# Fillers set by TensorE's trailing load, table loads begun in pauses, rounding moved to VectorE, and a new order of a fused attention and feed-forward kernel

## The chip, the cores and the metric

One core of a Trainium2 chip. The metric is the device time of one execution in microseconds, as the median of several runs. TensorE (PE) multiplies matrices, VectorE (DVE) and ScalarE (ACT) work on tiles, GpSimd (POOL) does some additions, and SyncE (SP) issues the DMAs. L748 is line 748 of the kernel.

## The reference

Inputs are q, k, v of 4 batches, 8 heads, 576 positions, 64 per head, and two weights of 512 x 2048 and 2048 x 512, all float32.

```python
q_d, k_d, v_d = (a.reshape(B, H, Sd, 4, D).mean(axis=3) for a in (q, k, v))
out_up = np.repeat(sm_attn(q_d, k_d, v_d), 4, axis=2)
mask = np.abs(pos[:, None] - pos[None, :]) < 4
scores = np.where(mask, scale * np.matmul(q, k.transpose(0, 1, 3, 2)), -1e9)
out_local = np.matmul(softmax(scores), v)
x = (out_up + out_local).transpose(0, 2, 1, 3).reshape(B * S, H * D)
h = x @ w_in
g = h * np.tanh(softplus(h))
return g @ w_out
```

So there are two attentions, one over means of four positions and one over a band of seven neighbours; their sum goes through two dense layers with Mish between them. 2304 rows of 512 come out.

## The kernel before

Work comes in units of one batch and one pair of heads, 16 in all. A unit loads q and k (`qk`) and v (`vv`), sums groups of four (L391), computes coarse scores `sc` (L406) and band scores `sl` (L445, some with the mask added by a matmul, L440), takes both softmaxes, transposes the probabilities (`at` with the remainder `Ar` at L489 and L490, `pt` and `pve` at L517 and L523), evicts them on ScalarE (`AT` L493, `R` L496, `PT` L520 and L524), multiplies by the values (`pvo` L504 and L508, the band's products L532), adds both on VectorE (L545) and splits the result into a rounded word and its remainder (L563 on ScalarE, L565 on VectorE). The remainder block `R` is 96 x 2 x 144 with three blocks of 16 rows on its diagonal; three ScalarE copies write them, and the rest was set to zero once.

Each weight tensor of 128 x 512 arrives as 64-bit words; ScalarE and VectorE turn their halves into one float (L596, L598, L600), ScalarE rounds the float to a high word (L603), and VectorE subtracts for the low word (L604). A product of two such split numbers is three matmuls.

The dense layers go in columns of 384 rows (`c`) and blocks of 128 hidden features (`f`, 16 of them). For columns 0 and 1 a slot is one (c, f): twelve matmuls into a hidden bank `h` (L748), of which there are two; Mish on ScalarE (L772), the rounded word `g` (L774), the remainder on VectorE (L775), and nine matmuls into three output banks `acc` (L788). The later columns are done four at a time by a scheme with seven products instead of eight (L709, L716).

The four units of batch 0 are the prologue; they use their own tiles and banks. The dense layers' banks and the weights with f of 5 and more take memory that the prologue leaves. The other units are spread over the first 32 slots. Exp and Mish need different tables on ScalarE; a table load stands before the first instruction that needs another table.

No order is written by hand. `Plan.order` (L162) runs through all operations with assumed durations and emits, per engine, the ready operation of the lowest priority number; each engine then executes its queue in that order. Priorities come from constants at the top: `ATT` and `UNIT` for the units, `WPRI`, `WACT` and `WDMA` for weights, `LAG` for output groups behind their slot. Where TensorE has nothing ready, the planner may insert a filler, a matmul of 128 x 512 on the identity (L885) into a bank that is used for nothing. Whether it does so was decided by the columns multiplied so far in the running period of fixed length `TICK` of the planner's time:

```python
o, when = None, max(1700, min((k + 1) * TICK, k * TICK + hot.get(k, 0) * TICK / (PACE * BUSY) - 299))
if when <= t < 1e6:
    o, when = self.fill(t), t + 100
```

Of the kernel before, what the change touches and what calls it, by code (L numbers as in the profile page):

```python
# [19 lines left out]
P = 128  # L20
BIG = 1e30
CH = 384
LAG = (5.03, 6.42, 5.0)
FA = 5
SETS = 3
ATT = {0: (-811.4, 62.2), 1: (-43.2, 13.7), 2: (1.5, 0.3), 3: (9.2, 7.8)}
WPRI = (-7.19, 1.09, 7.26)
UNIT = {(0, 0): 6, (0, 2): -4, (1, 2): 3, (0, 3): 20, (1, 0): -3, (1, 3): -29, (1, 1): 10, (0, 1): -22, (3, 2): -4, (3, 3): -1, (2, 1): 2, (2, 0): -9, (2, 2): 3, (2, 3): 7, (3, 0): -1, (3, 1): 3}
WARM = True
NPRO = 4  # L30
WACT = 33
# [6 lines left out]
PMASK = (0,)  # L38
AMUL = ((1, 0), (1, 2), (1, 3))
AEXP = ((0, 2), (1, 0), (1, 3))  # L40
NMISH = (4,)
TAIL = 0
SPRE = 34
SPRE2 = 65
JPRE = 17
XDMA = 2
QPRE = 36
QPRE2 = 87
QSTEP = 0.6
QDMA = -37  # L50
SUMS = 2
TPRE = 49
UPRE = -7
KEEP = 50
LOAD = 1350
TICK, BUSY, PACE = 3413.3, 3060, 1.6
KW = 38
RATE, LAND = 415.0, 1100
PAGE, FIRST, FETCH = 256, 193, (3200, 6000)
# [34 lines left out]
class Plan:  # L94
# [59 lines left out]
    def heat(self, hot, t, dur, cols):  # L154

        k = int(t // TICK)
        while dur and k * TICK < t + dur:
            part = min(t + dur, (k + 1) * TICK) - max(t, k * TICK)
            hot[k] = hot.get(k, 0) + cols * part / dur
            k += 1  # L160

    def order(self):  # L162
        import heapq
        for o in self.ops:
# [7 lines left out]
        dma, hot, parked, gap = 0.0, {0: 1000}, {}, 0  # L172
# [5 lines left out]
        while events:  # L178
# [3 lines left out]
            for e in pending:  # L182
# [12 lines left out]
                while ready[e]:  # L195
# [34 lines left out]
                    if e == "pe":  # L230
                        k = int(t // TICK)
                        if hot.get(k - 1, 0) < BUSY:
                            dur = o.cold
# [8 lines left out]
                        self.heat(hot, t, dur, o.cols)  # L242
                        for b in o.bufs:
                            b.todo -= 1
                    elif e == "act" and o.tab and o.tab != tab:
                        dur, tab = dur + max(0, LOAD - (t - free[e])), o.tab
# [3 lines left out]
                    if e == "sp":  # L250
                        late = t > 1e5
                        dma = max(dma, t + LAND + 400 * late) + o.dur * (1 + 0.28 * late)
                        free[e], end = max(t + 420, dma - DQ), dma
# [25 lines left out]
                if e == "pe" and self.filler and free[e] <= t:  # L279
                    k = int(t // TICK)  # L280
                    o, when = None, max(1700, min((k + 1) * TICK, k * TICK + hot.get(k, 0) * TICK / (PACE * BUSY) - 299))
                    if when <= t < 1e6:
                        o, when = self.fill(t), t + 100
# [4 lines left out]
                    if o:  # L288
                        o.end = free[e] = t + (o.cold if hot.get(k - 1, 0) < BUSY else o.dur)
# [27 lines left out]
class Kernel:  # L317
# [10 lines left out]
    def consts(self, pool):  # L328
# [625 lines left out]
```

## Time and profile before

| | us |
|---|---|
| median of 3 runs | 511.86 (511.3 to 512.08) |
| the profiled execution | 512.84 |
| its span, first to last instruction | 511.1 |
| TensorE busy in it | 490.2 |
| VectorE busy | 357.9 |
| ScalarE busy | 293.3 |

The profile is of one execution. Times in it count from the first instruction, and the execution's own time is 1.7 us longer than the span. Busy time is the union of an engine's instructions; two neighbouring instructions overlap a little, so the mean of one is longer than its distance to the next. PEclk is the granted TensorE clock, 1.00 for 2.4 GHz and 0.50 for 1.2 GHz.

### The profile page before, as it was taken

Reading aid. Unit: us, or ns where it says so; the run is one execution under the profiler, and the core shown is the slowest. Engines: PE = TensorE matmul, PEld = TensorE weight load, DVE = VectorE, ACT = ScalarE, POOL = GpSimd, SP = SyncE. Lnnn points to the kernel's source line nnn. Section 1 sums busy time; section 2 is a strip of 40 time slices with the busy share of each in tenths; the row PEclk is TensorE's granted clock in tenths of the full one; section 3 lists DMA queues with packets and bytes.
Section 4 is the critical chain, followed back from the end, with each engine's and each line's share of the span. In section 5 each row is a group of like instructions: output and inputs, shape, how many; then the busy total and the mean of one; then the engine's idle time right before and its main releaser. Section 6 shows DMA issues by size and latency. Waiting matters only on the chain.

```text
span 511.1 us, 11643 instructions
## 1 busy us (share of the span) xinstructions
PE 490.2 (96%) x4743; PEld 416.4 (81%) x4743; DVE 357.9 (70%) x804; ACT 293.3 (57%) x708; POOL 40.5 (8%) x62
## 2 busy tenths in 40 slices
PE   8788899999999999999999999999999999999997
PEld 3555778787977888887788988899888998889885
DVE  5796599999646676657898885666948676566442
ACT  2597799979855665856574433344735444344422
POOL 6400120010101111101100000000000000000000
PEclk9995899999999999999999999999999999999999
DMA  8974999240543677744230320100512000000003
GB/s 347 415 283 145 381 379 380 79 172 1 172 131 85 230 245 261 240 156 167 75 107 17 104 84 17 31 1 15 140 39 101 0 1 0 2 0 1 0 1 123
DMA packets 23381, 65.60 MB, mean 128 GB/s; under 512 B 2592, under 2 KB 12832, under 8 KB 21280
## 3 DMA queue, kind: packets, MB, share of 16 engines
q1 hardware_dynamic: 23328, 64.86, 35.4%
q8 instruction: 37, 0.61, 0.5%
q14 instruction: 16, 0.13, 0.1%
HBM read 53.84 MB, written 11.01 MB: 127 GB/s over the span
## 4 chain that ended last, share of the span: by engine, by line
PE 71%; ACT 12%; DVE 7%; DMA 6%; issue 2%; SPq 1%; POOL 0%; ACTq 0%; POOLq 0%; DVEq 0%
PE acc L788 32%; PE h L709 22%; PE h L748 7%; DMA raw_wi<-in_w_in_dram 3%; PE pve L532 3%; ACT A L413 2%; DMA vv<-in_vv_dram 1%; ACT raw_wo L596 1%; ACT L413 1%; PE pt L517 1%; DMA qk<-in_qk_dram 1%; ACT L772 1%; PE warm L885 1%; PE sc L406 1%; ACT raw_wi L596 1%
## 5 line engine op out<-in xcount | busy, mean ns | idle before, releaser
L788 PE MATMUL acc<-wo,g 128*128 128x512 f32 x864 | 223.7, 395 | 0.0
L788 PEld LDWEIGHTS acc<-wo,g 128*128 128x128 f32 x864 | 159.0, 188 | 26.8 <-issue 0.6
L716 DVE TENSOR_TENSOR u<-h,u 128x384 f32<-128x384 f32 x112 | 61.7, 554 | 30.9 <-PE h L709 30.2
L748 PE MATMUL h<-x,wi 128*128 128x384 f32 x384 | 79.1, 348 | 2.8 <-ACT mA L772 2.3
L748 PEld LDWEIGHTS h<-x,wi 128*128 128x128 f32 x384 | 68.0, 192 | 8.4 <-ACT mA L772 4.4
L772 ACT ACTIVATE u<-u 128x384 f32<-128x384 f32 (+1 forms) x66 | 33.9, 515 | 52.9 <-DVE u L716 52.9
L775 DVE TENSOR_TENSOR g<-u,g 128x384 fp32r<-128x384 f32 (+1 forms) x66 | 35.8, 543 | 38.5 <-ACT g L774 38.4
L774 ACT ACTIVATE g<-u 128x384 fp32r<-128x384 f32 (+1 forms) x66 | 33.8, 514 | 37.2 <-PE acc L788 36.3
L681 ACT ACTIVATE t<-b 128x256 fp32r<-128x256 f32 x64 | 26.3, 416 | 43.9 <-PE h L709 40.5
L709 PE MATMUL h<-x,t 128*128 128x384 f32 x192 | 41.3, 339 | 1.0 <-DVE u L716 1.0
L709 PE MATMUL h<-x,wi 128*128 128x384 f32 x192 | 40.4, 338 | 0.0
L709 PEld LDWEIGHTS h<-x,t 128*128 128x128 f32 x192 | 34.5, 188 | 4.1 <-DVE u L716 1.7
L478 POOL TENSOR_TENSOR vv<-vv 128x512 f32<-128x512 f32 x16 | 21.2, 1322 | 201.9 <-DMA vv<-in_vv_dram 167.1
L709 PEld LDWEIGHTS h<-x,wi 128*128 128x128 f32 x192 | 34.5, 188 | 2.2 <-issue 0.2
L709 PE MATMUL h<-sfar,t 128*128 128x384 f32 x144 | 31.3, 336 | 0.0
L678 DVE TENSOR_TENSOR b<-b,b 128x256 f32<-128x256 f32 x64 | 27.0, 422 | 1.1
L709 PEld LDWEIGHTS h<-sfar,t 128*128 128x128 f32 x144 | 25.7, 188 | 2.1
L672 DVE TENSOR_TENSOR b<-wi 128x256 f32<-128x256 f32 x64 | 26.3, 421 | 1.0
L391 DVE TENSOR_REDUCE qkd<-qk 128x288 f32<-128x1152 f32 x16 | 21.4, 1339 | 7.9 <-DMA qk<-in_qk_dram 7.8
L682 DVE TENSOR_TENSOR t<-b,t 128x256 fp32r<-128x256 f32 x64 | 26.5, 416 | 0.0
L532 PEld LDWEIGHTS pve<-PT,vv 38*64 38x64 f32 x640 | 22.4, 145 | 4.5 <-issue 1.2
L775 DVE TENSOR_TENSOR g<-mA,g 128x384 fp32r<-128x384 f32 x32 | 18.7, 587 | 8.7 <-ACT g L774 8.6
(106 smaller groups left out, 699.1 us busy)
## 6 DMA issues: line engine op xcount, KB each, us to landing
vv<-in_vv_dram SPq DMA_DIRECT2D x16, 1152.0 KB, 5.8
qk<-in_qk_dram SPq DMA_DIRECT2D x16, 582.0 KB, 6.5
raw_wi<-in_w_in_dram SPq DMA_DIRECT2D x16, 512.0 KB, 10.8
raw_wo<-in_w_out_dram SPq DMA_DIRECT2D x16, 512.0 KB, 9.9
out_dram<-o SPq DMA_DIRECT2D x18, 256.0 KB, 2.2
sa<-far SPq DMA_DIRECT2D x16, 192.0 KB, 2.7
fars<-sa SPq DMA_DIRECT2D x16, 192.0 KB, 1.9
q<-fars SPq DMA_DIRECT2D x16, 192.0 KB, 2.8
```

Of the source, the lines that this page charges most:

```text
L532: nc.tensor.matmul(o_()[64 * h:64 * h + 64, c0:c0 + 32], vw()[64 * e:64 * e + KW, j, f, 64 * h:64 * h + 64], PT()[64 * e:64 * e + KW, j, 6 ...
L672: op("dve", dve(n), lambda k=k, w=w, c=c: nc.vector.tensor_tensor(out=t[k](), in0=w()[:, 0, c:c + n].bitcast(F32), in1=w()[:, 1, c:c + n]. ...
L678: op("dve", dve(n), lambda ko=ko, a=a, b_=b_: nc.vector.tensor_tensor(out=t[ko](), in0=t[a](), in1=t[b_](), op=ALU.subtract), r=[t[a], t[b ...
L681: op("act", act(n), lambda w=w, ko=ko: nc.scalar.activation(w()[:, 0], t[ko](), AF.Copy), r=[t[ko]], w=[(w, 0)])
L682: op("dve", dve(n), lambda w=w, ko=ko: nc.vector.tensor_tensor(out=w()[:, 1], in0=t[ko](), in1=w()[:, 0].bitcast(F32), op=ALU.subtract), r ...
L709: nc.tensor.matmul(bank()[:, :CH], wv(a, j), xv()[:, b_], start=j == 0 and m == 0, stop=j == 1 and m == 2)
L716: op("dve", dve(CH), lambda: nc.vector.tensor_tensor(out=at[to](), in0=bank()[:, :CH], in1=at[a](), op=ALU.add), r=[bank] + u[a] * (a != t ...
L748: nc.tensor.matmul(h()[:, :CH], w()[:, a, kt * P:(kt + 1) * P], x()[:, b_, :], start=kt == 0 and j == 0, stop=kt == 3 and j == 2)
L772: op("act", act(n, psum), lambda o_=o_: nc.scalar.activation(Gv()[:, o_], Hv()[:, o_], AF.Mish), r=h_, w=x_, tab="mish")
L774: op("act", act(n), lambda o_=o_: nc.scalar.activation(g()[:, 0, o_], Gv()[:, o_], AF.Copy), r=x_, w=[one])
L775: op("dve", dve(n), lambda o_=o_: nc.vector.tensor_tensor(out=g()[:, 1, o_], in0=Gv()[:, o_], in1=g()[:, 0, o_].bitcast(F32), op=ALU.subtr ...
L788: nc.tensor.matmul(a_(), g()[:, a, i * P:(i + 1) * P], wo()[:, b_], start=first and j == 0, stop=last and j == 2)
```

## The change

Six parts:

1. A filler is now set wherever TensorE has nothing ready and the load of the last `TICK` of time, counted back from the present moment (`load`), is below `PACE`. The columns of several operations are counted anew, and columns at the low clock count twice.
2. Where ScalarE pauses longer than `PRE` ahead of an instruction that needs the other table, the plan puts an instruction on a 128 x 1 dummy there, which waits for nothing and needs that table; the load then stands before the dummy.
3. Nine high words of weights (`WHI`) and thirteen of activations (`GHI`) are rounded by VectorE instead of ScalarE.
4. In nine units (`RDV`) VectorE writes the whole remainder block at once, as the product of the transposed tile with a mask `diag` of zeros and ones that GpSimd builds at the start.
5. A softmax's small constant of 1e-9 is summed along as one more column of the tile `L` instead of being added by an instruction of its own.
6. All constants of the order are new. Masks are added by a matmul in batches 0 and 1 (`PMASK`), and other units scale on ScalarE (`AMUL`, `AEXP`).

```diff
-LAG = (5.03, 6.42, 5.0)
+LAG = (0.33, 3.75, 19.55)
...
-PMASK = (0,)
-AMUL = ((1, 0), (1, 2), (1, 3))
-AEXP = ((0, 2), (1, 0), (1, 3))
+PMASK = (0, 1)
+AMUL = ((0, 2), (0, 3), (1, 0), (1, 1), (1, 3))
+AEXP = ((0, 2), (1, 2))
+WHI = ((0, 'wo'), (4, 'wo'), (7, 'wi'), (8, 'wi'), (12, 'wi'), (12, 'wo'), (13, 'wo'), (14, 'wo'), (15, 'wo'))
+RDV = ((0, 1), (0, 2), (0, 3), (1, 3), (2, 2), (2, 3), (3, 0), (3, 1), (3, 2))
+GHI = (9, 10, 11, 13, 14, 15, 18, 21, 22, 24, 25, 29, 31)
...
-TICK, BUSY, PACE = 3413.3, 3060, 1.6
+TICK, BUSY, PACE = 3413.3, 3900, 4900
...
+        if dur:
+            self.trail.append((t, t + dur, cols / dur))
+
+    def load(self, t):
+
+        while self.trail and self.trail[0][1] < t - TICK:
+            self.trail.popleft()
+        return sum(r * (min(b, t) - max(a, t - TICK)) for a, b, r in self.trail if b > t - TICK and a < t)
...
-                        dur, tab = dur + max(0, LOAD - (t - free[e])), o.tab
+                        idle, tab = t - free[e], o.tab
+                        if idle > PRE:
+                            first = Op()
+                            first.eng, first.dur, first.fn, first.bufs, first.deps, first.outs = e, PRE + LOAD, self.preload[tab], [], None, []
+                            first.end, first.tab = free[e] + PRE + LOAD, tab
+                            out.append(first)
+                        dur += max(0, LOAD + (PRE - idle if idle > PRE else 0))
...
-                    o, when = None, max(1700, min((k + 1) * TICK, k * TICK + hot.get(k, 0) * TICK / (PACE * BUSY) - 299))
-                    if when <= t < 1e6:
-                        o, when = self.fill(t), t + 100
+                    o, when = None, max(1700, t + 120)
+                    if 1700 <= t < 1e6 and self.load(t) < PACE:
+                        o = self.fill(t)
...
-        for m in range(3):
-            op("act", act(96, True), lambda m=m: nc.scalar.activation(
-                R()[32 * m:32 * m + 16, :, 48 * m:48 * m + 48],
-                pa()[32 * m:32 * m + 16, 384:512].rearrange("p (h i) -> p h i", h=2)[:, :, :48], AF.Copy), r=[pa], w=[(R, m)])
+        if (b, p) in RDV:
+            op("dve", dve(288), lambda: nc.vector.tensor_tensor(
+                out=R().rearrange("p h (m i) -> p h m i", m=3),
+                in0=pa()[:96, 384:512].rearrange("p (h i) -> p h i", h=2)[:, :, None, :48].broadcast_to([96, 2, 3, 48]),
+                in1=self.diag[:, None].broadcast_to([96, 2, 3, 48]), op=ALU.mult), r=[pa], w=[R], two=False)
+        else:
...
+            if s in GHI:
+                op("dve", dve(n, True), lambda o_=o_: nc.vector.tensor_copy(g()[:, 0, o_], Gv()[:, o_]), r=x_, w=[one])
```

What the order became, at three places. In a name such as `PT_2_763` the first number is the pair of heads, the last one counts tiles.

ScalarE in the prologue, at the evictions `PT` of pairs 2 and 3 (`raw_...` are weights' halves, `xd` the coarse output, `wi` a rounded weight). Before:

```order
L596 ACTIVATE raw_wo_516<-raw_wo_516 128x512
L496 ACTIVATE R_att<-at_3_667 16x2x48
L596 ACTIVATE raw_wo_532<-raw_wo_532 128x512
L496 ACTIVATE R_att<-at_3_667 16x2x48
L596 ACTIVATE raw_wo_571<-raw_wo_571 128x512
L596 ACTIVATE raw_wo_629<-raw_wo_629 128x512
L413 ACTIVATE A_0_761,cst_0_736<-sc_0_680,cst_0_736 128x144
L520 ACTIVATE PT_2_763<-pt_2_741 128x512
L524 ACTIVATE PT_2_763<-pve_2_750 38x128
L512 ACTIVATE xd_3_774<-pvo_3_752 128x144
L413 ACTIVATE A_0_761,cst_0_736<-sc_0_680,cst_0_736 128x144
L520 ACTIVATE PT_3_817<-pt_3_766 128x512
```

Now:

```order
L630 ACTIVATE raw_wi_389<-raw_wi_389 128x512
L630 ACTIVATE raw_wo_439<-raw_wo_439 128x512
L546 ACTIVATE xd_2_656<-pvo_2_637 128x144
L554 ACTIVATE PT_3_658<-pt_3_646 128x512
L448 ACTIVATE A_3_601<-A_3_601,cst_3_551 128x128 x3
L554 ACTIVATE PT_2_679<-pt_2_665 128x512
L558 ACTIVATE PT_2_679<-pve_2_674 38x128
L558 ACTIVATE PT_3_658<-pve_3_654 38x128
L640 ACTIVATE wi_693<-full_wi_663 128x512
L630 ACTIVATE raw_wi_444<-raw_wi_444 128x512
L521 ACTIVATE AT_3_735<-at_3_688 128x288
L630 ACTIVATE raw_wo_492<-raw_wo_492 128x512
```

The first weight halves on ScalarE now are the two at the head of this piece, with eight more behind it; before, nine stood ahead of the second `PT`.

TensorE where the dense layers begin (`h` is a hidden bank, `acc` an output bank, `warm` the fillers' bank). Before, behind nine other fillers:

```order
L885 LDWEIGHTS ident
L885 MATMUL warm<-ident 128x512
L748 MATMUL h_914<-x_0_514,wi_641 128x384 x3
L748 MATMUL h_914<-x_0_653,wi_641 128x384 x3
L748 MATMUL h_914<-x_0_871,wi_641 128x384 x3
L748 MATMUL h_914<-x_0_885,wi_641 128x384 x3
L489 MATMUL at_0_945<-ident,A_0_761 128x128 x3
L490 MATMUL at_0_945<-ident,Ar_att 96x128
L748 MATMUL h_952<-x_0_514,wi_863 128x384 x3
```

Now, behind four fillers and the twelve matmuls of the first bank and six of the second:

```order
L785 MATMUL h_920<-x_0_752,wi_762 128x384 x3
L785 MATMUL h_920<-x_0_860,wi_762 128x384 x3
L927 LDWEIGHTS ident
L927 MATMUL h_958<-ident 128x128
L828 MATMUL acc_0_961<-wo_685,g_947 128x512 x3
L828 MATMUL acc_1_971<-wo_685,g_947 128x512 x3
L828 MATMUL acc_2_979<-wo_685,g_947 128x512 x3
L828 MATMUL acc_0_961<-wo_868,g_956 128x512 x3
L828 MATMUL acc_1_971<-wo_868,g_956 128x512 x3
L828 MATMUL acc_2_979<-wo_868,g_956 128x512 x3
L785 MATMUL h_958<-x_0_529,wi_918 128x384 x3
```

Two hidden banks are followed by both of their output groups, ahead of the third hidden bank. Before, four hidden banks and a whole attention unit came ahead of the first output group. The fillers ahead of the first hidden matmul of all number 49 before and 32 now.

ScalarE at the coarse Exp of pair 2 of batch 1, some way into the dense layers. Before:

```order
L772 ACT_TABLE_LOAD
L772 ACTIVATE mA_1473<-h_1297 128x384
L772 ACTIVATE mA_1491<-h_1392 128x384
L774 ACTIVATE g_1495<-mA_1473 128x384
L413 ACT_TABLE_LOAD
L413 ACTIVATE A_2_1503,cst_2_1475<-sc_2_1423,cst_2_1475 128x144
L603 ACTIVATE wo_1523<-full_wo_1493 128x512
```

Now:

```order
L640 ACTIVATE wo_1518<-full_wo_1506 128x512
L597 ACTIVATE x_1_634<-x_1_1_1567 128x192
L918 ACT_TABLE_LOAD
L918 ACTIVATE dummy<-one 128x1
L440 ACTIVATE A_2_1624,cst_2_1575<-sc_2_1560,cst_2_1575 128x144 x3
```

The load stands with the dummy, ahead of the Exp that waits for its maximum. There are 34 loads now and 32 before; 18 of the 34 stand with a dummy, none of them among the first eight behind the prologue.

## Rows read from the trace of the kernel before

**Rows 1.** The page: busy time of each engine, its share of the span, instructions.

```profile
PE 490.2 (96%) x4743; PEld 416.4 (81%) x4743; DVE 357.9 (70%) x804; ACT 293.3 (57%) x708; POOL 40.5 (8%) x62
```

**Rows 2.** Busy time by stretch: start:end, length, engines (x instructions), PEclk, DMA share, GB/s.

```profile
60.00:140.00 80.00, 77.84 (x968) 66.02 (x967) 70.03 (x149) 73.94 (x169) 9.35 (x8) 1.00 0.55 204
140.00:260.00 120.00, 116.38 (x1683) 97.33 (x1683) 79.75 (x176) 73.76 (x177) 14.48 (x14) 1.00 0.52 176
260.00:500.00 240.00, 239.03 (x1190) 214.81 (x1189) 163.97 (x371) 102.62 (x220) 0.00 (x0) 1.00 0.10 32
```

**Rows 3.** TensorE in order of time: start, us, operation [idle before <-releaser].

```profile
39.87 0.29 PE L523 MATMUL pve<-ident,L_att 128*38 128x128 f32 x1 [1.22 <-ACT PT L520]
...
45.09 4.45 PE L885 MATMUL warm<-ident 128*128 128x512 bf16 x10
49.60 0.69 PE L748 MATMUL h<-x,wi 128*128 128x384 f32 x1
```

**Rows 4.** Busy time by stretch again (PE, PEld, DVE, ACT, POOL), by clock steps.

```profile
36.82:40.23 3.41, 1.65 (x22) 0.86 (x21) 2.89 (x6) 3.34 (x10) 0.00 (x0) 1.00 0.60 175
40.23:50.47 10.24, 10.18 (x158) 6.51 (x156) 6.49 (x16) 7.79 (x33) 0.00 (x0) 0.50 0.42 132
53.88:57.30 3.42, 1.91 (x15) 1.12 (x14) 2.65 (x7) 3.36 (x7) 0.00 (x0) 1.00 1.03 419
57.30:60.71 3.41, 3.41 (x12) 3.26 (x13) 1.96 (x4) 3.04 (x8) 0.00 (x0) 0.50 1.02 411
```

**Rows 5.** Busy time by stretch of line 532 alone (PE, PEld), at pair 1, and at pairs 2 and 3.

```profile
21.00:22.30 1.30, 1.19 (x72) 1.19 (x72) 1.00 1.04 419
40.00:45.10 5.10, 4.54 (x144) 4.33 (x144) 0.52 0.01 3
```

**Rows 6.** VectorE at the end of the prologue, in order of time, and its busy time.

```profile
42.45 0.49 DVE L545 TENSOR_TENSOR x<-pve,xd 128x320 f32<-128x320 f32 x1 [2.74 <-PE pve L532]
...
45.21 0.49 DVE L545 TENSOR_TENSOR x<-pve,xd 128x320 f32<-128x320 f32 x1 [1.53 <-PE pve L532]
45.95 1.56 DVE L565 TENSOR_TENSOR x<-x,x 128x384 fp32r<-128x384 f32 x4
...
18.45:47.50 29.05, 22.94 (x65) 0.87 0.65 242
```

**Rows 7.** ScalarE in order of time: the eviction of pair 2's probabilities.

```profile
39.23 0.59 ACT L520 ACTIVATE PT<-pt 128x512 f32<-128x512 f32 x1
```

**Rows 8.** Groups by line and shape: xcount | busy us, mean ns | idle before <-releasers.

```profile
L413 ACT ACT_TABLE_LOAD x12 | 15.4, 1283 | 15.5 <-DVE cst L411 15.4
L774 ACT ACTIVATE g<-mA 128x384 fp32r<-128x384 f32 x32 | 16.6, 524 | 6.7 <-PE acc L788 6.5
L775 DVE TENSOR_TENSOR g<-mA,g 128x384 fp32r<-128x384 f32 x32 | 18.7, 587 | 8.7 <-ACT g L774 8.6
L603 ACT ACTIVATE wi<-full_wi 128x512 fp32r<-128x512 f32 x16 | 10.0, 625 | 0.1
L598 DVE TENSOR_SCALAR raw_wi<-raw_wi 128x512 int32<-128x512 int32 x16 | 6.5, 419 | 0.0
L496 ACT ACTIVATE R_att<-at 16x96 f32<-16x96 f32 x48 | 11.3, 235 | 0.6
```

**Rows 9.** Waits: engine, line and tile <- releaser: total us, times, longest.

```profile
PE h L748 <- ACT mA L772: 2.3, 2, 1.3
```

**Rows 10.** ScalarE in order of time at one table load.

```profile
148.95 1.28 ACT L413 ACT_TABLE_LOAD   x1 [3.72 <-DVE cst L411]
150.24 0.38 ACT L413 ACTIVATE A<-sc,cst 128x144 f32<-128x144 f32 x1
```

**Rows 11.** All engines in order of time at one wait of TensorE.

```profile
242.65 1.27 POOL L478 TENSOR_TENSOR vv<-vv 128x512 f32<-128x512 f32 x1 [11.34 <-DMA vv<-in_vv_dram]
242.72 1.27 DVE L427 TENSOR_TENSOR Ar_att<-A,cst 128x48 f32<-128x48 f32 x1
...
244.04 0.31 PE L490 MATMUL at<-ident,Ar_att 128*96 128x128 f32 x1 [1.04 <-DVE Ar_att L427]
```

More of the change, by code (lines that the diff above doesn't have):

```diff
@@ L231, in order @@
                         k = int(t // TICK)
-                        if hot.get(k - 1, 0) < BUSY:
+                        warm = hot.get(k - 1, 0) >= BUSY
+                        if not warm:
                             dur = o.cold
@@ L252, in order @@
                         dma = max(dma, t + LAND + 400 * late) + o.dur * (1 + 0.28 * late)
-                        free[e], end = max(t + 420, dma - DQ), dma
+                        free[e], end = max(t + 420, dma - DQ), dma + 600 * (late and o.dur < 800)
                     else:
@@ L288, in order @@
                     if o:
-                        o.end = free[e] = t + (o.cold if hot.get(k - 1, 0) < BUSY else o.dur)
+                        warm = hot.get(k - 1, 0) >= BUSY
+                        o.end = free[e] = t + (o.dur if warm else o.cold)
                         page -= o.ins
@@ L293, in order @@
                             came, page = free[e] + (FETCH[dma > t + 800]), page + PAGE
-                        self.heat(hot, t, free[e] - t, o.cols)
+                        self.heat(hot, t, free[e] - t, o.cols * (2 - warm))
                         out.append(o)
                         heapq.heappush(events, free[e])
-                    elif t < 1e6 and self.ops[-1].end is None:
-                        heapq.heappush(events, when)
+                    elif look <= t and self.ops[-1].end is None:
+                        look = when
+                        heapq.heappush(events, look)
         if sum(o.deps is not None for o in out) != len(self.ops):
@@ L346, in consts @@
             nc.gpsimd.memset(self.mask[64 * h + 32:64 * h + 64, T - 1, KW - 3:], -BIG)
+        self.diag = pool.tile([96, 3, 48], F32, tag="diag", name="diag")
+        nc.gpsimd.memset(self.diag, 0.0)
+        for m in range(3):
+            nc.gpsimd.memset(self.diag[32 * m:32 * m + 16, m], 1.0)
         self.one = pool.tile([P, 1], F32, tag="one", name="one")
@@ L876, in run @@
             self.quartet(64 + 4 * i, i, 4)
+        dummy = pools["stg"].tile([P, 1], F32, tag="dummy", name="dummy")
+        pl.preload = {k: (lambda f=f: nc.scalar.activation(dummy, self.one, f)) for k, f in (("exp", AF.Exp), ("mish", AF.Mish))}
         done = pl.gate = pl.op("pe", 0, lambda: None, after=gate, prio=-1000)
```

76 lines of the change are left out of this document (44 added, 32 removed).

## Prediction

> **What bounds the kernel now.** I read the page's first part, then stretches of 60 to 240 us, then the steps of the granted clock, then the time order on TensorE, VectorE and ScalarE around 45 us. TensorE is busy 490.2 of 511.1 us [rows 1]. From 260 to 500 us it is busy 239.03 of 240; from 60 to 260 us it stands still only 2.16 + 3.62 = 5.78 us [rows 2]. The matmuls of the two dense layers are the same in number in both kernels, so behind 60 us the end is the start of the dense layers plus a fixed sum of matmuls plus at most some 6 us of waits. What can move is the time until the first hidden-layer matmul (line 748), which starts at 49.60 us [rows 3].
>
> That start is late for a reason the rows show. In 36.82 to 40.23 us TensorE is busy 1.65 of 3.41 us, its lowest share there; right behind it the granted clock is 0.50 for 10.24 us, that is 1.2 GHz instead of 2.4, and again from 57.30 to 60.71 us behind a stretch with 1.91 of 3.42 busy [rows 4]. In the first slow stretch lie the value products (line 532) of the last two head pairs of the prologue: 4.54 us for both, against 1.19 us for one at full clock [rows 5]. VectorE waits for these products 2.74 and 1.53 us, and has written the last activations at 45.95 + 1.56 = 47.51 us [rows 6]. Yet ten fillers run from 45.09 for 4.45 us at half clock [rows 3], so that the first hidden matmul starts 49.60 - 47.51 = 2.1 us after its data is there. And why was TensorE idle before 40.23? It waited 1.22 us for the eviction of the transposed probabilities (PT, line 520) [rows 3], which stood behind weight instructions in ScalarE's queue and started only at 39.23 [rows 7].
>
> **The sum, step by step.** All against the profiled execution: span 511.1 us, 512.84 in all, 0.98 above the median of 511.86.
>
> Order of the prologue. In front of the two PT evictions the old queue holds nine weight instructions of line 596, the new one two of line 630; the rest follow behind them. So the products start earlier and VectorE's wait of 2.74 + 1.53 = 4.27 us goes. VectorE has nearly as much to do ahead of the last activations as before (fewer line-598 shifts and normalizations, more remainders and the mask products; under 1 us either way, left at zero), so its idle time is the most that can go: 29.05 - 22.94 = 6.11 us between 18.45 and 47.50 [rows 6]. With the 2.1 us behind the fillers (four stand there now, at the end of the prologue) the most is 8.2. I take 2.1 + 4.27 + 0.6 (a third of the other idle time) = **-7.0 us**; lower bound of the gain 2.1 + 1.1 = 3.2, the fillers and the slowness of one product (4.54 / 2 - 1.19). The loading of the weights with f of 5 and above is released when the prologue's memory is free, so it moves along; it costs nothing as long as the first ten weight tensors feed the first five slots.
>
> Begin of the dense layers. Now two output groups (line 828) follow the first two hidden banks at once, so TensorE waits for Mish of the first. From the end of the second bank to that I count a table load 1.28, Mish and the rounded part 0.52 each and the remainder 0.59 [rows 8], 2.9 us, and 0.1 for what ScalarE must finish ahead of the load: 3.0 us. Before, TensorE waited for Mish twice, 2.3 us in all [rows 9]. **+0.7 us**, bounds 0 and +3. The half-clock step behind it stays as it was: 3.41 us at half clock cost 1.7 [rows 4], in both kernels.
>
> Table loads in ScalarE's pauses. A load today waits with its instruction: line 413's twelve loads of 1283 ns stood behind 15.4 us of waiting for VectorE's maximum [rows 8], as at 148.95 [rows 10], where Exp starts 1.29 us after the load does. Eighteen of 34 loads now stand with an instruction that waits for nothing; each such wait gives back up to 1.28 us on the way to TensorE. But only those count that TensorE feels, and of its 5.78 us of waits the best seen is not of this kind: at 242.72 a product of 48 elements takes 1.27 us beside GpSimd's addition of 1.27, and TensorE waits 1.04 for it [rows 11]. **-1.0 us**, bounds 0 and -3.9 (the 5.78 less two such waits near 1). The Trainium skill (ScalarE: Activation LUTs, What ACT_TABLE_LOAD costs) gives 1283 ns for the load and 1380 more for a drain at each change of the set. The trace agrees on the load and shows no drain, since Exp starts 1.29 us after it. By the page the two loads more would cost ScalarE 5.3 us and not 2.6, and each wait saved would return 2.66; the row decides, and the sum stays.
>
> Words rounded on VectorE. 9 weights and 13 activations leave ScalarE: 9 x 0.63 + 13 x 0.52 = 12.4 us of it [rows 8]. No row shows a float copy on VectorE between SBUF tiles; the nearest are the one-source shift of 512 (0.42) and the two-source subtraction of 384 (0.59) [rows 8], so 22 of them cost 9 to 13 us. I take 0.42, as the copy has one source. The remainder block by a mask takes 27 ScalarE instructions of 0.24 (6.3 us) [rows 8] and puts nine products of 288 on VectorE, 0.5 each between the same neighbours. So VectorE gets some 14 us and ScalarE loses some 19. VectorE's cover: it is busy 70.03 of 80 us from 60 to 140 and 79.75 of 120 behind [rows 2]; ScalarE 73.94 of 80. About a third falls into the first stretch, which VectorE can hold (75 of 80), and ScalarE gets air. **0 us**, bounds -2 and +3; if the cover went, 5 us of VectorE would stand on the path. A rule speaks against these casts: the Trainium skill (SBUF — State Buffer, SBUF: two separate sides) says that VectorE in its two-port modes and GpSimd lock each other out of one port pair for a whole instruction. The trace agrees (1.27 beside 1.27) [rows 11]. By that rule 22 more such instructions, with GpSimd busy 23.83 of 200 us [rows 2], meet it three times and lose some 2 us on VectorE; that lies within the bounds.
>
> Rest. Two mask matmuls more (line 467) of 342 columns: a filler of 512 takes 0.445 at half clock, so 0.22 at full [rows 3], and with its weights I put 0.3 each: **+0.6 us**. A later output group per slot in the last third and the end itself (last group, eviction, one store) keep their form: 0. GpSimd's mask for the remainder is built ahead of the first copy of the attention mask, and five fillers stand at the start instead of eight; both act before 10 us, where VectorE later waits for the third and fourth pair's input anyway: 0, bounds 0 and +2.
>
> Sum: -7.0 + 0.7 - 1.0 + 0 + 0.6 = **-6.7 us**; 511.86 - 6.7 = 505.2 us.
>
> **Rivals.**
> *The clock falls as before or more.* 32 fillers instead of 49 in the prologue; between the first and the second pair's products there is none. If a read or an eviction comes late there, a stretch like 36.82 to 40.23 comes again and the products run at 1.2 GHz. For: the clock fell twice so in this kernel, both times behind waits for ScalarE [rows 3, 4, 9]. Against: fillers are now set wherever the last stretch was thinly loaded, and the PT wait is gone. Then only 3.2 of the 7.0 us come: 509.0 us.
> *More than that.* The start gains its cap of 8.2 and of the 5.78 us of waits some 4 go, because ScalarE has 19 us less to do. For: ScalarE is the fuller engine at 60 to 140 us. Against: two of the waits are GpSimd's. 505.2 - 1.2 - 4 = 500 us.
> *Slower: the wait for Mish takes the place.* Lag 0.33 instead of 5.03 puts each output group right behind its hidden bank, and only two banks exist. In the new order three such pairs follow each other. If each waits the 3.0 us of the first, this is 6.0 more than I count, and each drops the clock behind it as at 57.30 [rows 4]: three steps of 1.7 instead of one, 3.4 more. 505.2 + 9.4 = 514.6 us; it decides from 6.7 us of such waits on. For: each pair needs the other table. Against: while ScalarE changes tables, TensorE has attention work and further hidden banks to do.
>
> **How the numbers follow.** Forecast 0.50, clock 0.20, more 0.19, slower 0.11. About 0.2% (1 us) is what a measurement of this kernel can tell from no change. The forecast's own bounds are some 501 to 509; the range runs from the "more" case to just past the clock case, 499.7 to 510.5, and leaves out the slower case and the ends of the two others. Faster by over 0.2% is nearly all of the first three, 0.87; slower 0.09; the same 0.04, where the clock case and a mild form of the wait meet.
>
> **What would show it.** Right: the first hidden matmul (line 785) near 42.5 us; no ten fillers ahead of it; VectorE's idle time before the last activations down to some 2 us; the granted clock at 1.00 through the value products; line 440's loads without a wait in front, the waits at the dummies' line instead; TensorE from 260 us on as dense as now. Wrong: the first hidden matmul past 47 us; half-clock stretches before 40 us; TensorE waiting over 4 us for Mish between 42 and 75 us; VectorE at 78 of 80 us there, with output groups waiting for the remainder. If the start comes near 42.5 and the end does not, the time went into waits between 60 and 260 us, which must then exceed 5.78.

## The result, and the profile after

The changed kernel takes 505.06 us (median of 4 runs, 503.54 to 506.49) against 511.58 (510.76 to 512.08): ratio 0.9874, interval 0.9842 to 0.9906. Timed again beside its variants it came out at 0.984 (0.9808 to 0.9872); that ratio leaves out one slow execution of 510.54 us. So it is some 6 to 8 us faster; 505.2 had been forecast. The profiled execution took 505.01 us, with a span of 503.2.

The page of the changed kernel, busy time of each engine (answers to [rows 1]):

```profile
PE 482.8 (96%) x4729; PEld 415.0 (82%) x4729; DVE 360.8 (72%) x818; ACT 280.5 (56%) x668; POOL 40.8 (8%) x70
```

Busy time by stretch of the changed kernel (PE, PEld, DVE, ACT, POOL, then PEclk, DMA share, GB/s), to be held against [rows 2, 4, 6]:

```profile
60.00:140.00 80.00, 75.55 (x967) 63.88 (x966) 67.89 (x150) 58.62 (x151) 8.37 (x8) 0.98 0.50 182
140.00:260.00 120.00, 118.04 (x1699) 102.36 (x1698) 87.12 (x197) 79.88 (x178) 14.75 (x14) 1.00 0.53 179
260.00:500.00 240.00, 238.82 (x1184) 212.92 (x1182) 156.22 (x357) 98.97 (x216) 0.00 (x0) 1.00 0.11 34
...
26.59:30.00 3.41, 3.13 (x69) 2.03 (x71) 3.15 (x13) 3.13 (x17) 0.00 (x0) 0.84 1.02 405
30.00:33.42 3.42, 3.42 (x22) 2.65 (x21) 3.42 (x11) 2.69 (x8) 0.00 (x0) 0.66 0.97 379
57.31:60.72 3.41, 1.14 (x5) 1.13 (x5) 3.10 (x7) 3.38 (x7) 0.00 (x0) 0.84 1.02 407
60.72:64.13 3.41, 3.41 (x14) 3.27 (x14) 3.21 (x8) 2.02 (x7) 0.00 (x0) 0.66 1.02 407
...
18.45:42.80 24.35, 22.19 (x544) 15.82 (x540) 22.71 (x62) 20.84 (x71) 2.52 (x3) 0.93 0.72 281
```

VectorE now stands still for 24.35 - 22.71 = 1.64 us of the last part of the prologue, where it was 6.11 [rows 6]. The half clock holds for 6.8 us (28.9 to 32.3 and 59.6 to 63.0 by the stretches) and not for 10.24 + 3.41 us [rows 4]. ScalarE has gone from 73.94 to 58.62 us of the 80 from 60 to 140, and yet TensorE stands still longer there: 4.45 us and not 2.16.

TensorE of the changed kernel in order of time, at the start of the dense layers (answers to [rows 3]):

```profile
41.29 1.04 PE L927 MATMUL warm<-ident 128*128 128x512 bf16 x4
42.38 4.44 PE L785 MATMUL h<-x,wi 128*128 128x384 f32 x24
47.50 0.22 PE L927 MATMUL h<-ident 128*128 128x128 bf16 x1 [0.67 <-ACT mA L809]
48.20 4.52 PE L828 MATMUL acc<-wo,g 128*128 128x512 f32 x18 [0.49 <-ACT g L814]
59.59 3.92 PE L785 MATMUL h<-x,wi 128*128 128x384 f32 x12 [2.27 <-ACT mA L809]
```

The first hidden matmul starts at 42.38 us, where it was 49.60: 7.22 earlier. The last matmul ends at 499.43 and not at 507.25: 7.82 earlier. By this pair of profiles nearly all of the gain lies ahead of the first hidden matmul, and the rest changed by 0.6 us. The experiments show that this reading is too simple.

What TensorE waits for in the changed kernel (total us, times, longest; answers to [rows 9]):

```profile
PE pvo L538 <- POOL vd L508: 3.3, 3, 1.7
PE h L785 <- ACT mA L809: 2.9, 2, 2.3
...
PE at L518 <- DVE Ar_att L454: 1.6, 1, 1.6
```

The first is new: TensorE is there before GpSimd has summed v. From 60 to 260 us TensorE stands still for 4.45 + 1.96 = 6.41 us and not for 5.78.

Groups by line and shape in the changed kernel (answers to [rows 8]):

```profile
L815 DVE TENSOR_TENSOR g<-mA,g 128x384 fp32r<-128x384 f32 x32 | 21.1, 665 | 8.7 <-ACT g L814 8.5
L812 DVE CAST g<-mA 128x384 fp32r<-128x384 f32 x13 | 5.2, 399 | 3.2 <-PE acc L828 1.8 <-ACT mA L809 1.4
L524 DVE TENSOR_TENSOR R_att<-at,diag 96x288 f32<-96x288 f32 x9 | 4.1, 451 | 2.0 <-ACT AT L521 1.8
L638 DVE CAST wo<-full_wo 128x512 fp32r<-128x512 f32 x6 | 2.5, 419 | 0.0
L918 ACT ACT_TABLE_LOAD x18 | 23.1, 1283 | 0.3
L440 ACT ACT_TABLE_LOAD x2 | 2.6, 1283 | 1.2 <-DVE cst L438 1.2
```

The prices taken for the copy (0.42) and the mask product (0.5) hold on average: 0.40 to 0.42 and 0.45. The coarse Exp's loads no longer stand behind 15.4 us of waiting.

### The profile page after: what moved, and what is told of

Read it like the earlier page. It is cut to its first block, busy times and chain, and to the rows that moved or that the text cites. A ratio compares the mean times of both kernels' runs of the same rounds, so it can differ in the third digit from the quotient of the medians.

```text
span 503.2 us, 11610 instructions
## 1 busy us (share of the span) xinstructions
PE 482.8 (96%) x4729; PEld 415.0 (82%) x4729; DVE 360.8 (72%) x818; ACT 280.5 (56%) x668; POOL 40.8 (8%) x70
## 4 chain that ended last, share of the span: by engine, by line
PE 79%; DMA 8%; ACT 7%; DVE 3%; POOL 2%; issue 1%; POOLq 0%; SPq 0%
PE acc L828 35%; PE h L746 24%; PE h L785 9%; DMA vv<-in_vv_dram 4%; PE pve L566 2%; DMA raw_wi<-in_w_in_dram 2%; PE sc L433 2%; PE sl L472 2%; PE pt L551 1%; DMA far<-x 1%; PE pvo L538 1%; PE pvo L566 1%; POOL vv L506 1%; ACT raw_wi L630 1%; PE pvo L542 1%
## 5 line engine op out<-in xcount | busy, mean ns | idle before, releaser
L828 PE MATMUL acc<-wo,g 128*128 128x512 f32 x864 | 219.1, 395 | 0.5 <-ACT g L814 0.5
L785 PE MATMUL h<-x,wi 128*128 128x384 f32 x384 | 76.6, 347 | 2.9 <-ACT mA L809 2.9
L746 PE MATMUL h<-x,wi 128*128 128x384 f32 x192 | 41.3, 338 | 0.0
L746 PE MATMUL h<-x,t 128*128 128x384 f32 x192 | 39.0, 338 | 0.6 <-DVE u L753 0.6
L815 DVE TENSOR_TENSOR g<-mA,g 128x384 fp32r<-128x384 f32 x32 | 21.1, 665 | 8.7 <-ACT g L814 8.5
L566 PEld LDWEIGHTS pve<-PT,vv 38*64 38x64 f32 x640 | 21.1, 135 | 3.4 <-ACT PT L558 1.2
```

What stands on the lines that cost most here:

```text
L566: nc.tensor.matmul(o_()[64 * h:64 * h + 64, c0:c0 + 32], vw()[64 * e:64 * e + KW, j, f, 64 * h:64 * h + 64], PT()[64 * e:64 * e + KW, j, 6 ...
L746: nc.tensor.matmul(bank()[:, :CH], wv(a, j), xv()[:, b_], start=j == 0 and m == 0, stop=j == 1 and m == 2)
L785: nc.tensor.matmul(h()[:, :CH], w()[:, a, kt * P:(kt + 1) * P], x()[:, b_, :], start=kt == 0 and j == 0, stop=kt == 3 and j == 2)
L815: op("dve", dve(n), lambda o_=o_: nc.vector.tensor_tensor(out=g()[:, 1, o_], in0=Gv()[:, o_], in1=g()[:, 0, o_].bitcast(F32), op=ALU.subtr ...
L828: nc.tensor.matmul(a_(), g()[:, a, i * P:(i + 1) * P], wo()[:, b_], start=first and j == 0, stop=last and j == 2)
```

## The experiments

Twelve runs, each with the recorded order of its kernel and one edit of it, so that nothing else is planned anew. `find` looks up an operation by its engine and tiles, `move` puts operations ahead of (0) or behind (1) another one in the emitted list. The runs came in three sets on different chips, and each ratio is to executions of the kernel before in the same set, so ratios are compared and not medians; one hundredth is 5.1 us.

| run | edit | median us | ratio, 95% interval |
|---|---|---|---|
| after_again | none | 503.89 | 0.9840, 0.9808 to 0.9872 |
| a_nodummy | table loads back with their instruction | 506.68 | 0.9899, 0.9869 to 0.9930 |
| a_castact | 22 rounded words back on ScalarE | 507.71 | 0.9919, 0.9890 to 0.9948 |
| a_castfirst | the first of the 22 back | 506.26 | 0.9880, 0.9840 to 0.9921 |
| a_rcopy | remainder block by ScalarE copies | 507.43 | 0.9892, 0.9840 to 0.9944 |
| a_ptlate | evictions behind weight instructions | 507.02 | 0.9919, 0.9896 to 0.9941 |
| a_nofill | no fillers in the prologue | 504.47 | 0.9863, 0.9820 to 0.9906 |
| a_hoist | Mish ahead of three weight instructions | 505.37 | 0.9875, 0.9835 to 0.9914 |
| b_nofill | before, no ten fillers | 510.52 | 0.9983, 0.9956 to 1.0010 |
| b_ptearly | before, evictions early | 510.23 | 0.9954, 0.9932 to 0.9977 |
| b_both | before, both | 511.24 | 0.9989, 0.9962 to 1.0016 |
| b_ptdummy | before, evictions early, loads in pauses | 504.84 | 0.9855, 0.9807 to 0.9902 |

**The start: what moves it, and what it is worth.** In the kernel before, two edits:

```diff
# b_nofill
+        extra = [o for o in order if o.deps is None and o.cols == 512]
+        for o in extra[-10:]:
+            order.remove(o)
# b_ptearly
+        move([find("act", n) for n in ("raw_wi4", "raw_wo0", "raw_wo1", "raw_wo2", "raw_wo3")], find("act", "pve0_3", "PT0_3"), 1)
+        move([find("dve", "raw_wo0", "full_wo0"), find("dve", "raw_wo1", "full_wo1")], find("dve", "pvo0_2", "xd0_2"), 1)
```

> The kernel before, without the last ten fillers, which stand ahead of its first hidden matmul. Theory FILL (the matmul stood 2.1 us behind its data only because of them): the first hidden matmul starts at 47.5 us, 509.5 in all. Rival CLOCK (without them the load behind the value products is too thin, and the half clock lasts longer): the start moves forward by 2 us but the matmuls behind it stay at half clock for another step, which costs 1.7 us: 511 to 512.

> The kernel before, with five weight instructions of ScalarE (line 596) moved from ahead of the evictions of the transposed probabilities of pairs 2 and 3 to behind them, and two of VectorE's that read them (line 600) behind the first sum of pair 2. Theory EVICT (these nine instructions made the eviction late, this starved TensorE, and the clock fell): the eviction starts near 36.7 us instead of 39.23, no half clock from 40 us, VectorE's wait of 4.27 us goes; with the ten fillers still in place the first hidden matmul starts 2.5 to 5 us earlier: 506.5 to 509. Rival LATE (the eviction then waits for something else, or VectorE becomes the bound): under 1 us, 510.5 or above.

> Both edits of the kernel before together: no ten fillers, and the evictions ahead of the weight instructions. Theory FILL and EVICT together: start near 43 us, 504.5 to 506.5, the whole gain of the change. If they overlap: 507 to 508.5.

Moving the evictions does to the start what was said. TensorE of b_ptearly in order of time:

```profile
43.51 2.32 PE L748 MATMUL h<-x,wi 128*128 128x384 f32 x12 [0.41 <-DVE x L545]
...
48.68 0.32 PE L490 MATMUL at<-ident,Ar_att 128*96 128x128 f32 x1 [1.59 <-DVE Ar_att L427]
...
53.47 1.26 PE L748 MATMUL h<-x,wi 128*128 128x384 f32 x3 [1.34 <-ACT mA L772]
```

The first hidden matmul starts 6.1 us earlier, at full clock. But the kernel gains only 2.4 us by the ratio. Without the ten fillers (b_nofill) the start comes at 46.66, 2.9 us earlier, and the gain is 0.9 us, not told from nothing; b_both starts at 44.21 and gains no more than that. Where the start goes forward, the end hardly follows. In b_nofill part of the reason is its rival CLOCK, here in the stretch of the first twelve hidden matmuls:

```profile
46.66:51.20 4.54, 4.54 (x16) 4.44 (x16) 4.54 (x11) 4.45 (x18) 0.27 (x1) 0.51 0.95 345
```

They run at half clock and take 4.5 us, so that the second group starts 1.4 us earlier than before (51.2 and 52.6) and not 2.9. In b_both the clock is 0.50 from 42.8 to 49.6. A table of starts shows where the lead goes, in us, each the start of the n-th group of twelve hidden matmuls:

| | 1 | 2 | 3 | 11 | 15 | 19 | 21 | 32 | last matmul ends |
|---|---|---|---|---|---|---|---|---|---|
| before | 49.6 | 52.6 | 57.3 | 106.7 | 129.7 | 149.5 | 164.9 | 229.6 | 507.2 |
| b_ptearly | 43.5 | 48.7 | 53.5 | 102.9 | 126.5 | 146.3 | 163.8 | 228.3 | 505.8 |
| b_ptdummy | 43.8 | 49.0 | 53.7 | 102.0 | 125.6 | 145.3 | 158.5 | 221.0 | 496.7 |

In this pair of profiles 1.4 of 6.1 us are left at the end; of the rest, 2.5 are more standing still behind the first hidden matmul (10.79 us and not 8.27) and 2.1 more busy time (451.50 and not 449.38), some of it at half clock. By the table 2.2 go between the first two groups, at the 1.59 us wait for VectorE's remainder, and 2.1 between the 19th and the 21st. Busy time by stretch and, below, all engines in order of time in b_ptearly at that second place:

```profile
144.00:160.00 16.00, 13.65 (x180) 11.19 (x177) 8.88 (x18) 8.56 (x21) 2.34 (x2) 0.89 0.38 130
152.50:156.00 3.50, 3.50 (x11) 3.02 (x10) 1.54 (x5) 1.53 (x5) 0.00 (x0) 0.51 0.00 0
```

```profile
145.74 1.28 ACT L413 ACT_TABLE_LOAD   x1 [3.72 <-DVE cst L411]
147.04 0.38 ACT L413 ACTIVATE A<-sc,cst 128x144 f32<-128x144 f32 x1
...
149.58 1.42 POOL L478 TENSOR_TENSOR vv<-vv 128x512 f32<-128x512 f32 x1 [14.91 <-DMA vv<-in_vv_dram]
149.79 1.62 DVE L775 TENSOR_TENSOR g<-mA,g 128x384 fp32r<-128x384 f32 x1
...
151.33 0.72 DVE L427 TENSOR_TENSOR Ar_att<-A,cst 128x48 f32<-128x48 f32 x1
152.11 0.32 PE L490 MATMUL at<-ident,Ar_att 128*96 128x128 f32 x1 [1.58 <-DVE Ar_att L427]
```

ScalarE waits 3.72 us for the maximum and only then loads the table for 1.28; VectorE's work comes that much later and meets GpSimd's addition: the product just ahead of the remainder `Ar` takes 1.62 us (0.59 on average [rows 8]), `Ar` is late, TensorE waits, and runs at half clock for 3.4 us behind it.

**Table loads in pauses.** The same edit with dummies, and the change without its dummies:

```diff
# b_ptdummy, in addition to b_ptearly (o.gap: ScalarE's pause ahead of o in the plan, in ns)
...
+        tab, out = "exp", []
+        for o in order:
+            if o.eng == "act":
+                if o.tab and o.tab != tab:
+                    tab = o.tab
+                    if o.gap > 250:
+                        new = Op()
+                        new.eng, new.fn = "dummy", lambda f={"exp": AF.Exp, "mish": AF.Mish}[tab]: nc.scalar.activation(dummy, self.one, f)
+                        out.append(new)
+            out.append(o)
...
# a_nodummy
+        order = [o for o in order if o.fn not in pl.preload.values()]
```

> The kernel before with the evictions moved ahead of the weight instructions, as in the run that moved them alone, and with 12 dummies that begin table loads in ScalarE's planned pauses of over 250 ns, all behind 140 us. The evictions alone started the dense layers 6.1 us earlier, of which 2 to 2.4 us were left at the end; about 2 us went at 147 to 157 us, at a table load with a half-clock stretch behind it. Theory KEEP (the loads in pauses keep that part): 507.5 to 509. Rival ELSEWHERE (the loads are no part of it: the wait there is for the added maximum and the remainder on VectorE): 510 or above.

> The changed kernel in its own order, the 18 dummies left out, so that each table load stands with its instruction again. Theory START (the gain is the earlier first hidden matmul, the rest cancels): no load before 155 us is touched, so the start stays at 42.4 us, and behind it the loads cost TensorE 0 to 1.5 us: 505 to 506.5. Rival TABLE (the loads begun in pauses carry a part of the gain that other losses hide): 3 us or more slower than the changed kernel, 508 or above.

b_ptdummy, the same place, in order of time and by stretch:

```profile
140.82 0.26 ACT L525 ACTIVATE PT<-pve 38x128 f32<-38x128 f32 x1
141.10 1.28 ACT L911 ACT_TABLE_LOAD   x1
142.39 0.20 ACT L911 ACTIVATE dummy<-one 128x1 f32<-128x1 f32 x1
...
144.81 0.38 ACT L414 ACTIVATE A<-sc,cst 128x144 f32<-128x144 f32 x1 [2.21 <-DVE cst L412]
...
148.03 0.20 DVE L428 TENSOR_TENSOR Ar_att<-A,cst 128x48 f32<-128x48 f32 x1
...
148.44 0.27 PE L491 MATMUL at<-ident,Ar_att 128*96 128x128 f32 x1
148.76 1.29 POOL L479 TENSOR_TENSOR vv<-vv 128x512 f32<-128x512 f32 x1 [15.09 <-PE at L491]
```

```profile
144.00:160.00 16.00, 16.00 (x295) 14.00 (x282) 11.59 (x28) 11.41 (x32) 2.18 (x2) 1.00 0.60 193
```

The load is over before the maximum comes, `Ar` is written in 0.20 us ahead of GpSimd's addition, and TensorE is busy for all 16 us at full clock. From the evictions alone to this run the ratio falls from 0.9954 to 0.9855, some 5 us for twelve dummies of 0.2 us, more than theory KEEP expected. Of it this place shows about 4 us in the table of starts (a lead of 1.0 us at the 19th group, 5.3 at the 21st). The 9.1 us at the end of the two profiles say too much, since b_ptdummy's is one of its shortest executions and b_ptearly's one of its longest. These two edits give the kernel before as much as the whole change gives it. Taking the 18 dummies out of the changed kernel costs 1.3 to 3 us (against its two timings), between what START (0 to 1.5) and TABLE (3 or more) expected; the intervals overlap clearly with the first timing and hardly with the second. (The dummies there start at 98.3 us and not behind 155, as the expectation had it.) Why the loads cost less in that order was not tested.

**A late start without loss.** The changed kernel without its 32 fillers, and with its evictions late:

```diff
# a_nofill
+        order = [o for o in order if o.deps is not None or o.eng != "pe" or o.cols != 512]
# a_ptlate
+        move([find("act", n) for n in ("raw_wi1", "raw_wo1", "raw_wi2", "raw_wo2", "raw_wi3")], find("act", "pt0_3", "PT0_3"), 0)
```

> The changed kernel in its own order without the 32 fillers ahead of the first hidden matmul (they write to a bank that nothing reads). Theory CLOCK (the fillers hold the granted clock): long stretches at half clock before 40 us, the value products and the hidden matmuls behind them at half clock, the first hidden matmul 2 to 5 us later: 507 to 511. Rival LOAD (the prologue is bound by the loads and by VectorE, so TensorE's clock there costs nothing): 502 to 505.

> The changed kernel with five weight instructions of ScalarE (line 630) put back ahead of the evictions of the transposed probabilities of pairs 2 and 3. EVICT: 5 x 0.57 = 2.9 us of delay for the value products, and the clock falls as in the kernel before: the first hidden matmul 3 to 6 us later, 508 to 511. Rival SLACK (the evictions were not what the first hidden matmul waits for in the new order): 505 to 506.

Busy time by stretch of a_nofill: two stretches of the prologue at a low clock, and from the first hidden matmul to the end of the last; then the same of the changed kernel:

```profile
24.00:38.00 14.00, 13.38 (x173) 10.52 (x165) 10.20 (x33) 9.61 (x37) 0.00 (x0) 0.51 0.70 277
41.00:48.50 7.50, 6.25 (x164) 5.23 (x161) 6.54 (x15) 5.82 (x13) 0.00 (x0) 0.54 0.34 110
...
47.96:498.93 450.97, 446.21 (x3921) 391.14 (x3916) 324.74 (x739) 253.37 (x576) 26.16 (x24) 1.00 0.33 113
```

```profile
42.38:499.43 457.05, 446.60 (x3916) 391.67 (x3916) 327.60 (x739) 253.32 (x576) 25.53 (x24) 1.00 0.32 112
```

The clock falls in the prologue as theory CLOCK said (from 48.1 to 54.9 us it is back at 1.00, so that the first hidden matmuls do not suffer), and the first hidden matmul starts 5.6 us later. But the end does not move: the ratio of 0.9863 lies between the changed kernel's 0.9840 and 0.9874. LOAD had the time right and not the reason, since the prologue did become longer. From the first hidden matmul on TensorE stands still for 4.76 us and not for 10.45.

Where the lateness is repaid can be read from the starts: a_nofill is 4.9 us behind the changed kernel at the 11th group (106.8 and 101.9), 2.8 at the 15th (125.1 and 122.3) and 0.9 at the 19th (151.7 and 150.8). In that stretch the changed kernel waits 1.6 us for `Ar` at 106 us and 1.7 for GpSimd at 139 us, a_nofill for neither. The second wait goes with a load more than with the start. GpSimd sums a `v` whose load takes 7.5 us in the changed kernel and 5.7 in a_nofill. Of the nine profiled executions of this order and its variants, the six in which this load took 7.3 to 7.6 us have the wait (1.2 to 1.7), the three in which it took 5.5 to 5.7 have none, and their starts overlap (40.7 to 47.3 us and 43.8 to 48.0). So that a late start cost nothing is shown by the timings; that the waits repay it is shown in part.

Nor is every late start free: a_castact and a_rcopy, below, in which ScalarE has more to do, start at 46.48 and 47.34 and still stand for 10.63 and 10.60 us. a_ptlate starts at 45.28 and loses 2 to 4 us by its ratio, between its two theories; there ScalarE's weight instructions are moved too.

**Words and blocks off ScalarE.**

```diff
# a_castact (both lines), a_castfirst (the second for wo of f = 0 alone)
-                op("dve", dve(n, True), lambda o_=o_: nc.vector.tensor_copy(g()[:, 0, o_], Gv()[:, o_]), r=x_, w=[one])
+                op("dve", dve(n, True), lambda o_=o_: nc.scalar.activation(g()[:, 0, o_], Gv()[:, o_], AF.Copy), r=x_, w=[one])
...
-                op("dve", dve(512, True), lambda w=w, full=full: nc.vector.tensor_copy(w()[:, 0], full()), r=[full], w=[(w, 0)])
+                op("dve", dve(512, True), lambda w=w, full=full: nc.scalar.activation(w()[:, 0], full(), AF.Copy), r=[full], w=[(w, 0)])
# a_rcopy, in the RDV units; the lines of the mask product go
+            op("dve", dve(288), lambda: [nc.scalar.activation(
+                R()[32 * m:32 * m + 16, :, 48 * m:48 * m + 48],
+                pa()[32 * m:32 * m + 16, 384:512].rearrange("p (h i) -> p h i", h=2)[:, :, :48], AF.Copy) for m in range(3)], r=[pa], w=[R], two=False)
```

> The changed kernel once more, as the measure for its variants on the same chip. Every theory: 505.1 us, between 504 and 506.5, some 0.987 of the kernel before.

> The changed kernel in its own order, the 22 rounded words (9 weights, 13 activations) back on ScalarE at the same place of the plan. START: one of them lies ahead of the first hidden matmul, which moves by at most 0.6 us; the others have cover; 504.5 to 506. Rival CAST (ScalarE's relief of 12 us is what keeps the later slots dense): 508 or above. Rival PORT (VectorE loses to GpSimd by the casts): faster than the changed kernel, 503 to 504.

> The changed kernel in its own order with one rounded word of the 22, the prologue's (weight wo of f = 0, at 33 us), back on ScalarE. With all 22 back it came out about 3 us slower than the changed kernel. Theory FIRST (the one in the prologue does it: it stands ahead of the last eviction of the probabilities, makes TensorE wait and lowers its clock): 506.5 to 508.5, first hidden matmul at 44 us or later. Rival LATER (the 21 behind the prologue do it, by ScalarE's load): 503.5 to 505.5.

> The changed kernel in its own order, the nine remainder blocks written by three ScalarE copies each instead of by the mask product on VectorE. Theory CHAIN (the three copies stand one behind the other ahead of the matmuls that read the block, three times in the prologue alone): 1.5 to 3 us slower than the changed kernel, 505.5 to 508. Rival COVER (other work hides them): 503.5 to 505.5.

Rounding on ScalarE costs 2.3 to 4 us, against the changed kernel's two timings: theory CAST, though its 508 was not quite reached. The late start alone does not explain it: a_castact starts 1.5 us before a_nofill and ends 3.3 us behind it. TensorE's waits in a_castact, and the longest one behind 100 us:

```profile
PE h L785 <- ACT mA L809: 4.3, 3, 2.9
PE pvo L538 <- POOL vd L508: 2.2, 2, 1.6
PE pvo L566 <- issue: 1.7, 1, 1.7
...
141.82 0.47 PE L538 MATMUL pvo<-AT,vd 128*64 128x144 f32 x4 [1.59 <-POOL vd L508]
```

It waits for ScalarE's Mish 4.3 us and not 2.9, although it starts later. But that is not where a_nofill gets ahead: the 15th groups of the two start together (125.3 and 125.1 us) and the 19th at 154.8 and 151.7, and between them a_castact waits for GpSimd (1.59), without a releaser (0.74) and for `Ar` (0.37), not for Mish. The wait for GpSimd again goes with the load, 7.5 us here and 5.7 in a_nofill, issued at 131.7 and 131.5. So that the rounding costs time on ScalarE is shown by the timings; by which wait is not. The first word alone (a_castfirst) and the copies of the block (a_rcopy, 1 to 3 us slower by the ratios) lie inside the spread of the changed kernel's own timings; how the loss divides stays open.

**A repair that brought nothing.** The wait at 57.3 us stands behind weight instructions in ScalarE's queue:

```diff
# a_hoist
+        move([find("act", n) for n in ("raw_wi7", "raw_wo7", "raw_wi8")], find("dve", "raw_wi7", "full_wi7"), 0)
```

> The changed kernel with three weight instructions of ScalarE (line 630, the tensors of f = 7 and the first of f = 8) moved from ahead of the Mish of the third hidden bank to behind the fourth. Theory QUEUE (the 2.27 us wait at 57.3 us and the half-clock stretch behind it come from ScalarE's queue): the wait falls to under 0.5, the clock stays up, 501.5 to 503.5. Rival WEIGHT (the matmuls at 59.6 us would next wait for the low word of the fifth slot's weight, written until 58.5): at most 1.1 us of the wait goes and the clock falls all the same, 504 to 505.

TensorE of a_hoist in order of time, its waits from 55 to 80 us:

```profile
59.54 2.37 PE L785 MATMUL h<-x,wi 128*128 128x384 f32 x12 [0.87 <-ACT mA L809]
67.39 1.90 PE L828 MATMUL acc<-wo,g 128*128 128x512 f32 x7 [0.41 <-DVE g L815]
75.24 1.32 PE L785 MATMUL h<-x,wi 128*128 128x384 f32 x6 [0.95 <-ACT mA L809]
```

The wait falls from 2.27 to 0.87 and the clock stays up there, as QUEUE said, but its time does not come: 0.41 and 0.95 of waiting follow, and the eighth group of hidden matmuls starts 31.5 us behind the first, as it does in after_again (31.5; in the first profile, with its half clock there, 32.6). The time is not told from the changed kernel's. No run here beats both kernels clearly; the change with a better onset and b_ptdummy's order were not combined.

## Why the prediction was right, step by step

**Start, -7.0.** Right in place and in size: 42.38 us against 42.5 forecast, VectorE's idle time at 1.64, the evictions as the cause (b_ptearly moves them alone and gets 6.1 of it). Three other executions with the same prologue queues up to the first hidden matmul started at 40.71, 42.45 and 43.78, so one profile gives it to about 1.5 us. The 2.1 us put down to the ten fillers are no part of their own: without them b_both starts at 44.21, with them b_ptearly at 43.51.

**What failed is the step under it:** "behind 60 us the end is the start of the dense layers plus a fixed sum of matmuls plus at most some 6 us of waits". The matmuls are fixed in number, but neither the waits nor the clock behind them stay as they were when the start moves. b_ptearly keeps 2.4 of its 6.1 us by the ratio, and a_nofill, 5.6 us later, loses none. In the profiles of b_ptearly and the kernel before, 2.5 us went into waits and 2.1 into longer busy time. So -7.0 was right for the start and, taken alone, too much for the end; why a_nofill loses nothing is open in part.

**Table loads, -1.0.** Mis-sized: -5 in the kernel before with early evictions, -1.3 to -3 when undone in the changed one. The prediction had set aside the waits whose releaser was a product beside GpSimd's addition [rows 11]. The one near 150 us was late because a table load stood ahead of it: with the load in a pause b_ptdummy does not have that collision. Nor does it have the later one, where TensorE waits 1.04 us in the kernel before [rows 11] and in b_ptearly; but b_nofill, without dummies, lacks that one too. The load's own price held: 1283 ns, the load starts right behind ScalarE's last instruction (140.82 + 0.26, then 141.10 in b_ptdummy), and the dummy 1.29 us after it. The drain of 1380 ns that the Trainium skill states for a change of the set (ScalarE: Activation LUTs, What ACT_TABLE_LOAD costs) does not show here either.

**Words rounded on VectorE, 0 (bounds -2 and +3).** Mis-sized as well, and outside its bound of -2: undone, it costs 2.3 to 4 us. The prices of the copies were right and VectorE did hold them; what was left at nothing is what 12.4 us less on ScalarE are worth. What VectorE loses to GpSimd by it was put at some 2 us, an estimate from the lock between VectorE and GpSimd that the Trainium skill states (SBUF — State Buffer, SBUF: two separate sides). The trace agrees with the lock and makes it cheaper here:

```profile
163.25 1.29 POOL L506 TENSOR_TENSOR vv<-vv 128x512 f32<-128x512 f32 x1 [12.54 <-DMA vv<-in_vv_dram]
163.83 0.92 DVE L812 CAST g<-mA 128x384 fp32r<-128x384 f32 x1 [1.44 <-ACT mA L809]
```

The copies of 384 take 0.35 us alone, and this one, beside GpSimd, 0.92. The 22 copies meet GpSimd three times here, as estimated, and lose 0.6 us by it; in the second profile of the kernel they meet it twice and lose 0.9. The remainders `g` rose from 587 to 665 ns [rows 8], all of it in those that ran beside GpSimd (the others take 0.55 us in both kernels); in the second profile they are at 594, so this differs between executions and is not the copies' price.

**Begin of the dense layers, +0.7.** The first wait was 0.67 + 0.49 and not 3.0, since ScalarE's table load began at 45.66 us, before the second bank was through (46.82); the fifth group of hidden matmuls then waited 2.27 for the Mish of the third, with a half-clock stretch behind. Together 3.4 us against 2.3: +1.1, and the slower rival in a mild form.

**The sum, -6.7 (measured -6.5),** came out so closely by luck, because two errors stood against each other: the start was credited too much, the loads and the rounding too little. Undone one by one, the evictions, the loads, the rounding and the block cost about 3, 2, 3 and 2 us (the last not told from nothing); the parts meet in the same waits, so none of them has a share of its own.

**The clock rival** (509.0): its condition came about in part, its price did not. The clock did fall at 28.9 us in this execution, though not in the band's value products (line 566), and even some 24 us at half clock ahead of the first hidden matmul in a_nofill cost nothing at the end: the start came 5.6 us later, and TensorE stood still for 5.7 us less behind it. In the kernel before it was otherwise (b_nofill), where the half clock reached into the hidden matmuls.

## What to carry to other kernels

A start that moves forward is worth what the next waits leave of it: before crediting it in full, ask for each of the next waits whether its producer moves along, and whether the clock holds. A table load that stands behind a wait costs more than its 1.28 us where the delayed work then meets another engine or drops the clock; a tiny activation that waits for nothing, put into the pause ahead, is a cheap thing to try first. And when parts of a change are tried, undo them in the recorded order, one at a time, and expect their costs not to add up.

## What the runs showed of the hardware

Executions of one kernel differ by several us, the longer ones mostly at a lower mean granted clock: of the 29 executions of the kernel before beside b_nofill, the shortest took 508.49 us at a mean of 0.993 and the longest 514.8 at 0.983. The mean alone does not set the time: a_nofill took 503.78 us at 0.976. The half clock falls at other places in each execution: the changed kernel had two stretches of 3.4 us in one profile and none in the next.

Inside the value products of the prologue TensorE stood for 0.7 to 1.8 us with no releaser shown ("issue") in seven of the nine profiled executions of the changed order and its variants, with the DMA engines at a share of 1.0; in the five of the order before there was none. Two of them:

```profile
26.86 0.24 PE L566 MATMUL pvo<-PT,vv 38*64 38x32 f32 x2 [0.88 <-issue]
...
23.49 0.25 PE L566 MATMUL pvo<-PT,vv 38*64 38x32 f32 x2 [1.77 <-issue]
```

The place goes by the count of instructions and not by the work. Counted along TensorE's matmuls and weight loads in the trace, the first stands ahead of the 963rd, in the second set of value products, and so it does in five more executions. The second is a_nofill's, ahead of the 706th; in the other eight the 706th belongs to other matmuls (line 472), and there too TensorE stands without a releaser, for 0.2 to 1.4 us. The distance is 257. In seven of the nine it does so again at the 4034th or 4035th (0.3 to 0.7 us), about 12 x 256 further on. What TensorE waits for there stays open.
